# Left-over tokens of two experts share a tile: two column groups of the array, one expert in each

## The chip, the cores and the metric

The kernel runs on one core of one Trainium2 chip. The metric is the device time of one execution in microseconds (us). Times quoted are medians of the fast runs. A ratio is the mean time of one kernel's fast runs over that of the other's in the same rounds on the same chip, so it is not quite the ratio of the medians beside it. One profiled execution of each kernel gives the trace; what is told of a stage is read there.

## The reference, cut to what matters

Attention over 8 batches of 576 positions gives x, 4608 tokens of 512 features. Then each token goes to one of 8 experts, chosen by a gate and, for some tokens, inherited from the token before:

```python
for b in range(B):
    prev_e = -1
    for s in range(S):
        fresh_e = int(np.argmax(logits[b, s]))
        if s == 0 or local_gate[b, s] < 0.5:
            e = fresh_e
        else:
            e = prev_e if prev_e >= 0 else fresh_e
        prev_e = e
        # p = softmax(logits[b, s])
        h = np.maximum(x[b, s] @ w1[e], 0.0)      # 512 -> 1024
        out[b, s] = p[e] * (h @ w2[e])            # 1024 -> 512
```

All of it is float32. The weights of one expert are 2 x 2.1 MB.

## The kernel before

The kernel sorts the tokens by expert into tiles of 128. A tile holds tokens of one expert only, so each expert's count is rounded up to whole tiles. A first round of six tiles is made from the first three batches while attention still runs; the second round is routed during the first tiles. Each tile gathers its tokens, loads its expert's weights two tiles ahead into a ring of two, and runs two layers on TensorE (of a matmul's two operands, lhsT is called stationary and rhs moving). How many tiles there are is known only at run time; the last ones stand under an `If`.

```python
# route(): tiles of each expert, then small matmuls that spread the result
nc.vector.tensor_tensor(nti, ps[0:R, 0:1], nn[:, 0:1], op=Alu.add)     # count + 127
nc.vector.tensor_scalar(nti, nti, 7, None, Alu.arith_shift_right)
# ... cut ...
nc.tensor.matmul(ps[:, 0:n], lhsT=c.ones, rhs=over, start=True, stop=True)
# ... cut: for t in range(LT): slots of the tokens, six matmuls ...

# Experts
def hidden(self, j):                       # h transposed: W1 stationary, tokens move
    for g in range(FK // self.HB):
        ps = self.psh[2 * j + g]
        for i in range(self.HB):
            c = slice((g * self.HB + i) * P, (g * self.HB + i + 1) * P)
            for kk in range(DK):
                ins = nc.tensor.matmul(ps[:, i], lhsT=w1[:, kk, c], rhs=xT[:, kk * P:(kk + 1) * P],
                                       start=(kk == 0), stop=(kk == DK - 1))
        nc.scalar.activation(hT[:, g * self.HB:(g + 1) * self.HB], ps, Act.Relu)

def output(self, j):                       # tokens stationary, W2 moves
    for kk in range(FK):
        ins = nc.tensor.matmul(ps, lhsT=self.hT[j][:, kk], rhs=self.w2t[j][:, kk, :],
                               start=(kk == 0), stop=(kk == FK - 1))
    nc.scalar.activation(y, ps, Act.Copy, scale=self.pt[j])
    # ... cut: scatter of y to the output by an indirect DMA ...

def run(self, ctx, second, check):
    # ... cut ...
    for j in range(NT):
        ahead = self.weights(j + 2) if j + 2 < NT else []      # four pieces of 1 MB
        # ... cut: gather of tile j + 3; the last tiles under tc.If(used > ...) ...
        ins = self.hidden(j)
        for piece in ahead[:2]:
            piece()
        # ... cut: stages of the routing are put here while j < 3 ...
        if j + 1 < NT:
            self.turn_x(j + 1)             # four transposes
        ins = self.output(j)
        for piece in ahead[2:]:
            piece()
```

## Time and profile before

| what | value | read from |
|---|---|---|
| time | 773.4 us, 3 runs, 771.2 to 774.74 | runs |
| span of the profiled run | 775.6 us, granted clock 0.982 | core list |
| TensorE busy | 96% | page, part 1 |
| tiles run | 40 | matmul counts |
| one whole tile, start to start | 14.45 us | timeline |
| DMA in the expert stage (250 to 744 us) | share 0.91, 325 GB/s | windows |

A line of a costliest-groups list gives the source line, engine, operation, tile written and tiles read, shapes, count; then busy time and mean length of one; then the engine's idle time ahead of them and what ended it. Durations of matmuls overlap (a pass of the output layer lasts 0.59 us, and the next starts 0.43 us after it), so lengths of stages are taken from starts in the timeline. A line of a windows view gives the stretch and its length, then the busy time and number of instructions of PE (TensorE's matmuls), PEld (its weight loads), DVE (VectorE), ACT (ScalarE) and POOL (GpSimd), then the granted clock (the share of TensorE's full clock that it was given), the DMA share and GB/s. In float32 each matmul appears as two instructions, called passes (64 for the 32 matmuls of a hidden layer). The lines themselves are in the prediction.

### The profile page before, as it was taken

What the parts mean: (1) busy time and instruction counts of PE and PEld (TensorE: products, weight loads), DVE (VectorE), ACT (ScalarE), POOL (GpSimd) and SP (SyncE); (2) the same over time, 40 slices, a digit from 0 to 9 for tenths busy, and PEclk for the clock granted to TensorE, in tenths of its full rate; (3) what the DMA queues carried; (4) which work ended last, traced back from release to release, by engine and by line L of the source; (5) the groups of instructions that cost most, each with busy time, mean ns of one, the idle gap of its engine ahead of it and who ended that gap; (6) DMA issues with size and microseconds to landing.
All of it is one profiled execution on the core that took longest, in us unless ns stands there. A gap on an engine that the chain in (4) does not pass through costs nothing. (4 is left out here: it accounts for less than half of the span.)

```text
span 775.6 us, 13139 instructions
## 1 busy us (share of the span) xinstructions
PE 746.9 (96%) x5308; PEld 576.3 (74%) x5308; DVE 180.2 (23%) x599; ACT 151.9 (20%) x273; POOL 85.7 (11%) x104
## 2 busy tenths in 40 slices
PE   7999999999999999999999999999999999999990
PEld 7999889887777767767767767768768768768760
DVE  5677877753720000000000000000000000000000
ACT  2544434531101101101101101111111111111110
POOL 1000002001021111111111111111111111101100
PEclk9999979999999999999999999999999999999995
DMA  9888778886789899999899899899899899899892
GB/s 353 316 299 276 245 250 296 296 288 245 262 329 328 307 328 343 308 341 324 303 349 328 305 343 334 307 346 340 287 337 330 312 338 339 299 344 325 310 324 82
DMA packets 95977, 238.81 MB, mean 308 GB/s; under 512 B 10718, under 2 KB 19934, under 8 KB 95904
## 3 DMA queue, kind: packets, MB, share of 16 engines
q1 hardware_dynamic: 88736, 216.87, 79.5%
q0 software_dynamic: 6640, 20.89, 7.2%
q8 instruction: 46, 0.75, 0.4%
q14 instruction: 27, 0.22, 0.1%
q10 hardware_dynamic: 528, 0.07, 0.1%
HBM read 218.79 MB, written 20.07 MB: 308 GB/s over the span
## 5 line engine op out<-in xcount | busy, mean ns | idle before, releaser
L690 PEld LDWEIGHTS hps<-xgT,w1t 128*128 128x128 f32 x2560 | 291.7, 192 | 17.3 <-issue 16.7
L690 PE MATMUL hps<-xgT,w1t 128*128 128x128 f32 x2560 | 292.8, 275 | 0.3 <-DVE xgT L676 0.3
L699 PE MATMUL yps<-w2t,hT 128*128 128x512 f32 x640 | 281.3, 592 | 0.0
L699 PEld LDWEIGHTS yps<-w2t,hT 128*128 128x128 f32 x640 | 118.5, 190 | 133.9 <-issue 133.9
L676 DVE COPY xgT<-tps 128x512 f32<-128x512 f32 x41 | 28.3, 690 | 487.5 <-PE tps L675 487.3
L692 ACT ACTIVATE hT<-hps 128x512 f32<-128x512 f32 x80 | 47.8, 597 | 241.4 <-PE hps L690 238.4
L667 POOL DMA_INDIRECT xg<-xd,gi x43 | 42.0, 976 | 402.2 <-issue 144.9
L701 ACT ACTIVATE y<-yps,pt 128x512 f32<-128x512 f32 x40 | 27.5, 687 | 267.7 <-PE yps L699 267.7
L702 POOL DMA_INDIRECT out_dram<-y,si x40 | 40.5, 1011 | 268.0 <-ACT y L701 254.6
L315 PE MATMUL sps<-qt,kt 64*128 64x96 f32 (+2 forms) x704 | 50.7, 290 | 5.3 <-DMA kt<-in_k_dram 5.0
L315 PEld LDWEIGHTS sps<-qt,kt 64*128 64x128 f32 (+2 forms) x704 | 44.6, 197 | 10.0 <-issue 8.2
L319 ACT ACTIVATE e<-sps 128x576 f32<-128x576 f32 (+1 forms) x64 | 39.9, 651 | 19.4 <-PE sps L315 17.6
L362 PE MATMUL vps<-vlt,e 128*96 128x96 f32 x384 | 41.1, 265 | 0.0
L362 PEld LDWEIGHTS vps<-vlt,e 128*96 128x96 f32 x384 | 37.5, 177 | 3.9 <-issue 3.1
L362 PE MATMUL vps<-vst,e 108*108 108x108 f32 (+1 forms) x320 | 38.0, 274 | 1.0 <-DVE xs L373 0.8
L362 PEld LDWEIGHTS vps<-vst,e 108*108 108x108 f32 (+1 forms) x320 | 34.7, 185 | 2.7 <-PE vps L362 0.9
L322 DVE TENSOR_TENSOR e<-e,maskL 128x576 f32<-128x576 f32 x32 | 23.2, 753 | 18.3 <-ACT e L319 16.7
L322 DVE TENSOR_TENSOR e<-e,maskS 108x648 f32<-108x648 f32 (+1 forms) x32 | 23.1, 754 | 9.5 <-ACT e L319 9.5
L405 ACT COPY xT<-xps 128x324 f32<-128x324 f32 (+1 forms) x32 | 18.6, 683 | 33.0 <-PE xps L399 33.0
L675 PE MATMUL tps<-ident,xg 128*128 128x128 f32 x164 | 24.9, 273 | 0.0
L675 PEld LDWEIGHTS tps<-ident,xg 128*128 128x128 f32 x164 | 19.3, 142 | 0.1
L373 DVE TENSOR_TENSOR xl<-vps,rc 96x384 f32<-96x384 f32 x32 | 17.3, 545 | 0.5
(145 smaller groups left out, 230.9 us busy)
## 6 DMA issues: line engine op xcount, KB each, us to landing
w1t<-in_w_dram SPq DMA_DIRECT2D x84, 1024.0 KB
w2t<-in_w_dram SPq DMA_DIRECT2D x84, 1024.0 KB
kt<-in_k_dram SPq DMA_DIRECT2D x15, 608.0 KB
qt<-in_q_dram SPq DMA_DIRECT2D x15, 576.0 KB
vlt<-in_vl_dram SPq DMA_DIRECT2D x8, 780.0 KB
vst<-in_vs_dram SPq DMA_DIRECT2D x8, 650.0 KB
xd<-xl SPq DMA_DIRECT2D x8, 576.0 KB
xd<-xs SPq DMA_DIRECT2D x24, 108.0 KB
```

Source lines behind the costliest of these rows:

```text
L315: st["pe"] = nc.tensor.matmul(ps[0:kb, h, i * w:(i + 1) * w], lhsT=kt[r, u.i2, c:c + kb], rhs=qt[r, u.i2, c:c + w], start=True, stop=True)
L319: nc.scalar.activation(ev, ps[0:kb, :, 0:m * w], Act.Exp, bias=0.0, scale=1.0 / DH ** 0.5)
L322: nc.vector.tensor_tensor(blocks(ev, m), blocks(ev, m), mask, op=Alu.mult)
L362: nc.tensor.matmul(ps[0:w, o:o + w], lhsT=u.e[0:kb, h, i * w:(i + 1) * w], rhs=vt[0:kb, u.i2, u.t0 + i, c:c + w], start=True, stop=True)
L667: self.nc.gpsimd.indirect_dma_start(out=self.xg[j], out_offset=None, in_=self.xd[0:t["rows"]], in_offset=bass.IndirectOffsetOnAxis(ap=t["r ...
L675: nc.tensor.transpose(ps[:, kk * P:(kk + 1) * P], x[:, kk * P:(kk + 1) * P], self.c.ident)
L676: ins = nc.vector.tensor_copy(self.xT[j], ps)
L690: ins = nc.tensor.matmul(ps[:, i], lhsT=w1[:, kk, c], rhs=xT[:, kk * P:(kk + 1) * P], start=(kk == 0), stop=(kk == DK - 1))
L692: nc.scalar.activation(hT[:, g * self.HB:(g + 1) * self.HB], ps, Act.Relu)
L699: ins = nc.tensor.matmul(ps, lhsT=self.hT[j][:, kk], rhs=self.w2t[j][:, kk, :], start=(kk == 0), stop=(kk == FK - 1))
L701: nc.scalar.activation(y, ps, Act.Copy, scale=self.pt[j])
L702: nc.gpsimd.indirect_dma_start(out=self.out, in_=y, in_offset=None, bounds_check=N - 1, oob_is_err=False, out_offset=bass.IndirectOffsetOn ...
```

## The change

The intent: rounding up wastes rows. An expert whose left-over is at most 64 tokens now takes only half of a tile, and two such experts share one. For the mixed tile TensorE's array is used as two column groups of 64: each group holds the tokens of one half, and each expert's weights move through its own group. There are two mixed tiles (four halves), at fixed places 14 and 25 in the list, and so fewer whole ones. The second expert's weights go to a buffer of their own, in four pieces spread over four earlier tiles.

```diff
+HT = P // 2
+NM = 2
+NH = 2 * NM
+NT_MIN = (N - E * HT) // P
+NT_MAX = max((N + E * (P - HT - 1)) // P, N // P - 1 + E - NH)
+NT = NT_MAX + NM
+MIXED = (14, 25)
# ... cut; route(): one stage more, and three small matmuls more in a later one ...
+    if final:
+        few, rank, half = nn[:, 6:7], nn[:, 7:8], nn[:, 8:9]
+        nc.vector.tensor_tensor(few, nt, nts[:, 1:2], op=Alu.subtract)
+        ps = bank()
+        nc.tensor.matmul(ps[0:R, 0:1], lhsT=c.less[0:E, 0:R], rhs=few[0:E], start=True, stop=True)
# ... cut ...
+        yield
# ... cut ...
-    nc.tensor.matmul(ps[:, 0:n], lhsT=c.ones, rhs=over, start=True, stop=True)
+    nc.tensor.matmul(ps[:, 0:whole], lhsT=c.ones, rhs=over, start=True, stop=True)
     if final:
         nc.tensor.matmul(ps[0:1, n:n + 1], lhsT=c.ones[:, 0:1], rhs=nt[0:E], start=True, stop=True)
+        nc.tensor.matmul(ps[0:1, n + 1:n + 1 + NH], lhsT=c.er[0:E], rhs=whose, start=True, stop=True)
+        for h in range(2):
+            nc.tensor.matmul(ps[:, whole:n], lhsT=c.half[h], rhs=whose.rearrange("e (m h) -> e h m", h=2)[:, h],
+                             start=(h == 0), stop=(h == 1))
# ... cut; Experts ...
+    def hidden_mixed(self, j):
+        nc, xT = self.nc, self.xT[j]
+        for f in range(2):
+            ps = self.bank().rearrange("p a b -> p (a b)")
+            for kk in range(DK):
+                for h, w1 in enumerate((self.w1t[j], self.w1x)):
+                    nc.tensor.matmul(ps[h * HT:(h + 1) * HT], lhsT=xT[:, kk * P + h * HT:kk * P + (h + 1) * HT],
+                                     rhs=w1[:, kk, f * 512:(f + 1) * 512], start=(kk == 0), stop=(kk == DK - 1))
+            nc.scalar.activation(self.h[:, f * 512:(f + 1) * 512], ps, Act.Relu)
+        return self.turn_h(j, 0)
# ... cut: turn_h, four transposes of h and a copy to hT ...
     def output(self, j):
+        if "halves" in t:
+            self.turn_h(j, 1)
+            for kk in range(FK):
+                for h, w2 in enumerate((self.w2t[j], self.w2x)):
+                    s = slice(h * HT, (h + 1) * HT)
+                    ins = nc.tensor.matmul(ps[s], lhsT=self.hT[j][:, kk, s], rhs=w2[:, kk, :],
+                                           start=(kk == 0), stop=(kk == FK - 1))
# ... cut; run() ...
+            if j + 6 in MIXED:
+                extra = self.weights(j + 6, 1)
# ... cut ...
-            for piece in ahead[2:]:
+            for piece in ahead[2:] + extra[:1]:
                 piece()
+            extra = extra[1:]
```

The routing now spreads over four tiles instead of three, and the gathers of tiles 6 and 7 wait until tile 4.

More of the change, by code (lines that the diff above doesn't have):

```diff
@@ L41 @@
 GC = 32
-NT = (N + E * (P - 1)) // P
-NT_MIN = N // P
+HT = P // 2
[5 more added lines that the diff above has]
+MIXED = (14, 25)
 SKIP = 8192
@@ L92, with __init__ @@
 class Round:
-    def __init__(self, pool, n):
-        self.n = n
-        self.gi = pool.tile([P, n], I32, name="gi")
-        self.si = pool.tile([P, n], I32, name="si")
-        self.oh = pool.tile([P, n, E], F32, name="oh")
-        self.et = pool.tile([1, n + 1], I32, name="et")
+    def __init__(self, pool, whole, nm=0):
+        self.whole, self.n = whole, whole + nm
+        self.gi = pool.tile([P, self.n], I32, name="gi")
+        self.si = pool.tile([P, self.n], I32, name="si")
+        self.oh = pool.tile([P, self.n, E], F32, name="oh")
+        self.et = pool.tile([1, self.n + 1 + 2 * nm], I32, name="et")
 @with_exitstack
@@ L162, in __init__ @@
         nc.vector.memset(self.ones, 1.0)
+        self.half = []
+        for h in range(2):
+            t = pool.tile([E, P], F32, name=f"half{h}")
+            nc.vector.memset(t, 0.0)
+            nc.vector.tensor_scalar(t[:, h * HT:(h + 1) * HT], self.ones[:, 0:HT], er[0:E], None, Alu.mult)
+            self.half.append(t)
         _, self.io = const([P, P], [[1, P]], 0, 0, "io")
@@ L173, in passes @@
         r2 = ctx.enter_context(tc.tile_pool(name="slots2", bufs=1))
-        r2 = Round(r2, NT - NE)
+        r2 = Round(r2, NT_MAX - NE, NM)
         codes = keep.tile([LQ, LT, B, E], F32, name="codes")
@@ L486, in route @@
     nc = tc.nc
-    R, CN, n = nb * E, LT * nb, rd.n
+    R, CN, n, whole = nb * E, LT * nb, rd.n, rd.whole
     final = nb == B
@@ L516, in route @@
     nc.tensor.matmul(ps[0:R, 1:2], lhsT=c.before[0:R, 0:R], rhs=cnt, start=True, stop=True)
-    nn = rp.tile([R, 8], F32, name="nn")
+    nn = rp.tile([R, 12], F32, name="nn")
     if final:
@@ L524, in route @@
         nc.vector.memset(nn[:, 0:1], 0.0)
-    nti = rp.tile([R, 1], I32, name="nti")
-    nc.vector.tensor_tensor(nti, ps[0:R, 0:1], nn[:, 0:1], op=Alu.add)
+    nti = rp.tile([R, 2], I32, name="nti")
+    nc.vector.tensor_tensor(nti[:, 0:1], ps[0:R, 0:1], nn[:, 0:1], op=Alu.add)
+    nc.vector.tensor_scalar(nti[:, 1:2], nti[:, 0:1], -float(HT), None, Alu.add)
     nc.vector.tensor_scalar(nti, nti, 7, None, Alu.arith_shift_right)
-    nt = rp.tile([R, 1], F32, name="nt")
-    nc.vector.tensor_copy(nt, nti)
+    nts = rp.tile([R, 2], F32, name="nt")
+    nc.vector.tensor_copy(nts, nti)
+    nt = nts[:, 0:1]
     yield
+    if final:
[3 more added lines that the diff above has]
+        nc.tensor.matmul(ps[0:R, 0:1], lhsT=c.less[0:E, 0:R], rhs=few[0:E], start=True, stop=True)
+        nc.vector.tensor_copy(rank, ps[0:R, 0:1])
+        nc.vector.scalar_tensor_tensor(half, rank, float(NH), few, Alu.is_lt, Alu.mult)
+        nc.vector.tensor_tensor(nt, nt, half, op=Alu.subtract)
+        whose = rp.tile([E, NH], F32, name="whose")
+        nc.vector.tensor_scalar(whose, c.io[0:E, 0:NH], rank[0:E], half[0:E], Alu.is_equal, Alu.mult)
+        yield
     ps = bank()
@@ L546, in route @@
     nc.vector.tensor_tensor(end, first[0:E], tiles[0:E], op=Alu.add)
-    over = rp.tile([E, n], F32, name="over")
-    nc.vector.tensor_scalar(over, c.io[0:E, 0:n], end, None, Alu.is_ge)
+    over = rp.tile([E, whole], F32, name="over")
+    nc.vector.tensor_scalar(over, c.io[0:E, 0:whole], end, None, Alu.is_ge)
     thr, base = nn[:, 4:5], nn[:, 5:6]
@@ L559, in route @@
     nc.vector.scalar_tensor_tensor(slot, cum, base, slot, Alu.add, Alu.add)
+    if final:
+        last, far = nn[:, 9:10], nn[:, 10:11]
+        nc.vector.scalar_tensor_tensor(last, nt, float(P), thr, Alu.mult, Alu.add)
+        nc.vector.tensor_tensor(far, first, nt, op=Alu.add)
+        nc.vector.tensor_scalar(far, far, -float(P), float(P * whole), Alu.mult, Alu.add)
+        nc.vector.scalar_tensor_tensor(far, rank, float(HT), far, Alu.mult, Alu.add)
+        more = rp.tile([R, S], F32, name="more")
+        nc.vector.tensor_scalar(more, cum, last, far, Alu.is_gt, Alu.mult)
+        nc.vector.tensor_tensor(slot, slot, more, op=Alu.add)
     nc.vector.tensor_tensor(slot, slot, hot, op=Alu.mult)
@@ L564, in route @@
     ps = bank()
-    nc.tensor.matmul(ps[:, 0:n], lhsT=c.ones, rhs=over, start=True, stop=True)
+    nc.tensor.matmul(ps[:, 0:whole], lhsT=c.ones, rhs=over, start=True, stop=True)
     if final:
         nc.tensor.matmul(ps[0:1, n:n + 1], lhsT=c.ones[:, 0:1], rhs=nt[0:E], start=True, stop=True)
+        nc.tensor.matmul(ps[0:1, n + 1:n + 1 + NH], lhsT=c.er[0:E], rhs=whose, start=True, stop=True)
+        for h in range(2):
+            nc.tensor.matmul(ps[:, whole:n], lhsT=c.half[h], rhs=whose.rearrange("e (m h) -> e h m", h=2)[:, h],
+                             start=(h == 0), stop=(h == 1))
     sp = bank()
@@ L573, in route @@
     if final:
-        nc.vector.tensor_copy(rd.et[:, n:], ps[0:1, n:n + 1])
+        nc.vector.tensor_copy(rd.et[:, n:], ps[0:1, n:n + 1 + NH])
     nc.vector.tensor_tensor(rd.oh, across(c.io[:, 0:E], [P, n, E]), spread(ps[:, 0:n], [P, n, E]), op=Alu.is_equal)
@@ L647, in __init__, with weights @@
         self.pt = Ring(xp, 2, [P, 1], "pt")
-        self.T = [dict(rd=r1, i=i, rows=BE * S) for i in range(NE)] + [dict(rd=r2, i=i, rows=N) for i in range(NT - NE)]
-    def weights(self, j):
+        self.T = [dict(rd=r1, i=i, rows=BE * S) for i in range(NE)] + [dict(rd=r2, i=i, rows=N) for i in range(r2.whole)]
+        for m, j in enumerate(MIXED):
+            self.T.insert(j, dict(rd=r2, i=r2.whole + m, rows=N, halves=[r2.n + 1 + 2 * m + h for h in range(2)]))
+        self.used = 0
+    def weights(self, j, h=0):
         nc, t = self.nc, self.T[j]
@@ L654, in weights, with load @@
         w2 = lambda e: self.w2[bass.ds(e, 1)].rearrange("o (k p) f -> p (o k) f", p=P)
-        def load(dst, src, h):
-            if "e" not in t:
-                t["e"] = nc.values_load(t["rd"].et[0:1, t["i"]:t["i"] + 1], engines=[ET.SP], min_val=0, max_val=E - 1,
-                                        skip_runtime_bounds_check_because="a count of at most 8 experts, held to 7")
+        at = t["halves"][h] if "halves" in t else t["i"]
+        def load(dst, src, part):
+            if ("e", h) not in t:
+                t["e", h] = nc.values_load(t["rd"].et[0:1, at:at + 1], engines=[ET.SP], min_val=0, max_val=E - 1,
+                                           skip_runtime_bounds_check_because="an expert, from 0 to 7")
             k = dst.shape[1] // 2
-            nc.sync.dma_start(out=dst[:, h * k:(h + 1) * k], in_=src(t["e"])[:, h * k:(h + 1) * k])
-        return [lambda a=a, h=h: load(*a, h) for a in ((self.w1t[j], w1), (self.w2t[j], w2)) for h in range(2)]
+            s = slice(part * k, (part + 1) * k)
+            nc.sync.dma_start(out=dst[:, s], in_=src(t["e", h])[:, s])
+        to = ((self.w1x, w1), (self.w2x, w2)) if h else ((self.w1t[j], w1), (self.w2t[j], w2))
+        return [lambda a=a, part=part: load(*a, part) for a in to for part in range(2)]
     def gather(self, j):
@@ L680, in turn_x, with bank, turn_h @@
             nc.vector.tensor_reduce(self.pt[j], self.pe[j], axis=AX.X, op=Alu.add)
+    def bank(self):
+        self.used += 1
+        return self.psh[self.used - 1]
+    def hidden_mixed(self, j):
[8 more added lines that the diff above has]
+        return self.turn_h(j, 0)
+    def turn_h(self, j, f):
+        nc, ps = self.nc, self.bank()
+        for i in range(self.HB):
+            k = f * self.HB + i
+            ins = nc.tensor.transpose(ps[:, i], self.h[:, k * P:(k + 1) * P], self.c.ident)
+        nc.vector.tensor_copy(self.hT[j][:, f * self.HB:(f + 1) * self.HB], ps)
+        return ins.ins
     def hidden(self, j):
@@ L685, in hidden @@
         for g in range(FK // self.HB):
-            ps = self.psh[2 * j + g]
+            ps = self.bank()
             for i in range(self.HB):
@@ L697, in output @@
         ps, y = self.psy[j], self.y[j]
-        for kk in range(FK):
-            ins = nc.tensor.matmul(ps, lhsT=self.hT[j][:, kk], rhs=self.w2t[j][:, kk, :],
-                                   start=(kk == 0), stop=(kk == FK - 1))
+        if "halves" in t:
[5 more added lines that the diff above has]
+                                           start=(kk == 0), stop=(kk == FK - 1))
+        else:
+            for kk in range(FK):
+                ins = nc.tensor.matmul(ps, lhsT=self.hT[j][:, kk], rhs=self.w2t[j][:, kk, :],
+                                       start=(kk == 0), stop=(kk == FK - 1))
         nc.scalar.activation(y, ps, Act.Copy, scale=self.pt[j])
@@ L712, in run @@
         self.psy = Ring(pp, 2, [P, D], "yps")
+        xp = ctx.enter_context(tc.tile_pool(name="mixed", bufs=1))
+        self.w1x = xp.tile([P, DK, F], F32, name="w1x")
+        self.w2x = xp.tile([P, FK, D], F32, name="w2x")
+        self.h = xp.tile([P, F], F32, name="h")
+        steps = NE - AHEAD + 1
         used = None
+        extra = []
         self.turn_x(0)
-        for j in range(NT):
+        for j, t in enumerate(self.T):
             ahead = self.weights(j + 2) if j + 2 < NT else []
-            if j + AHEAD < NT:
-                self.gather(j + AHEAD)
+            for g in [] if j == steps - 1 else [NE, NE + 1] if j == steps else [j + AHEAD]:
+                if g < NT:
+                    self.gather(g)
             if j == NE and check:
                 check()
-            if j >= NT_MIN:
+            if j + 6 in MIXED:
+                extra = self.weights(j + 6, 1)
+            if t["rd"] is self.r2 and NT_MIN - NE <= t["i"] < self.r2.whole:
                 if used is None:
-                    et = self.r2.et
-                    used = self.nc.values_load(et[0:1, NT - NE:], min_val=NT_MIN - NE, max_val=NT - NE,
-                                               skip_runtime_bounds_check_because="the sum of the experts' tiles")
-                ctx.enter_context(tc.If(used > j - NE))
-            ins = self.hidden(j)
+                    at = self.r2.n
+                    used = self.nc.values_load(self.r2.et[0:1, at:at + 1], min_val=NT_MIN - NE, max_val=NT_MAX - NE,
+                                               skip_runtime_bounds_check_because="the sum of the experts' whole tiles")
+                ctx.enter_context(tc.If(used > t["i"]))
+            ins = (self.hidden_mixed if "halves" in t else self.hidden)(j)
             for piece in ahead[:2]:
                 piece()
-            if j < NE - AHEAD:
+            if j < steps:
                 with tc.issue_after(ins):
                     next(second, None)
-                    if j == NE - AHEAD - 1:
-                        next(second, None)
             if j + 1 < NT:
@@ L737, in run @@
             ins = self.output(j)
-            for piece in ahead[2:]:
+            for piece in ahead[2:] + extra[:1]:
                 piece()
-            if j < NE - AHEAD:
+            extra = extra[1:]
+            if j < steps:
                 with tc.issue_after(ins):
```

## The prediction

> **What bounds the kernel now.** I read the page's busy rows and costliest groups first, then the windows of 50 us, then the timeline of one tile, then the DMA queue's issues.
>
> ```profile
> PE 746.9 (96%) x5308; PEld 576.3 (74%) x5308; DVE 180.2 (23%) x599; ACT 151.9 (20%) x273; POOL 85.7 (11%) x104
> ...
> L690 PE MATMUL hps<-xgT,w1t 128*128 128x128 f32 x2560 | 292.8, 275 | 0.3 <-DVE xgT L676 0.3
> L699 PE MATMUL yps<-w2t,hT 128*128 128x512 f32 x640 | 281.3, 592 | 0.0
> ```
>
> The two expert matmul groups hold 574 us of a 775.6 us span, with 0.3 us of idle ahead of them. A whole tile is 64 instructions of L690 and 16 of L699 (32 and 8 matmuls in float32, two passes each), so 2560/64 = 640/16 = 40 tiles ran. Busy times of matmuls overlap, so I take starts from the timeline of one tile in the middle (start, length, engine):
>
> ```profile
> 407.59 7.31 PE L690 MATMUL hps<-xgT,w1t 128*128 128x128 f32 x64
> ...
> 414.74 0.60 PE L675 MATMUL tps<-ident,xg 128*128 128x128 f32 x4
> ...
> 415.17 7.03 PE L699 MATMUL yps<-w2t,hT 128*128 128x512 f32 x16
> ...
> 422.04 7.31 PE L690 MATMUL hps<-xgT,w1t 128*128 128x128 f32 x64
> ```
>
> From start to start: hidden layer 414.74 - 407.59 = 7.15 us (112 ns a pass), four transposes 0.43 us, output layer 422.04 - 415.17 = 6.87 us (429 ns a pass of 512 columns). A tile is **14.45 us**, and the next begins at once. The other possible bound is the weights: 4.19 MB a tile. Windows of 1 us in that tile (the columns at the end are granted clock, DMA share, GB/s):
>
> ```profile
> 402.00:403.00 1.00, 1.00 (x4) 0.51 (x3) 0.00 (x0) 0.00 (x0) 0.57 (x1) 1.00 1.05 422
> ...
> 414.00:415.00 1.00, 1.00 (x12) 1.00 (x11) 0.00 (x0) 0.00 (x1) 0.00 (x0) 1.00 0.36 141
> ```
>
> ```profile
> 400.04 0.99 SPq L661 DMA_DIRECT2D w1t<-in_w_dram  x2
> 404.35 3.81 SPq L661 DMA_DIRECT2D w2t<-in_w_dram  x2
> 414.49 1.03 SPq L661 DMA_DIRECT2D w1t<-in_w_dram  x2
> ```
>
> The DMA is near full in the middle of a tile and falls off at its end, until a hidden layer frees the next w1 buffer: the queue waits for TensorE, not the reverse. The two are close (window 400:450: DMA share 0.90, 325 GB/s), so both must be checked. Adding up the packets of the weight queue, I find the last w2 piece of that tile landing at 416.4, the second w1 piece issued at 415.15 landing at 422.1, and its tile starting at 436.5: **14 us of slack**.
>
> [...] the gate matmuls (L415) put four results into four groups of 32 columns.
>
> ```profile
> 50.49 0.64 PEld L415 LDWEIGHTS xps<-xT,wgs 128*32 128x32 f32 x16
> 50.49 1.18 PE L415 MATMUL xps<-xT,wgs 128*32 128x288 f32 x16
> ```
>
> Sixteen passes of 288 columns one after the other would take 16 x 429 x 288/512 = 3.86 us; they took 1.18 us, and the starts come in fours, about 7 ns apart, 243 ns from four to four. So in this very data type the groups overlap fully[...]. [...] In the trace the matmul after the gates starts 0.09 us later than the last four's 243 ns would allow; I book 0.1 us a switch. [...] the trace shows 390 to 440 while pieces queue behind each other.
>
> **The change part by part.**
>
> *Tiles.* Running the reference's routing on its inputs gives 701, 469, 606, 495, 656, 452, 546 and 683 tokens for the eight experts; left over after whole tiles of 128: 61, 85, 94, 111, 16, 68, 34, 43. Rounded up that is 40 tiles, as the profile has. Experts 0, 4, 6 and 7 have at most 64 left over: exactly the four halves of two mixed tiles. So 36 whole and 2 mixed tiles: **four whole tiles (57.80 us) are replaced by two mixed ones.**
>
> *A mixed tile on TensorE.* The hidden layer swaps operands: the 64 tokens of each half are stationary, W1 moves in 512 columns. 2 x 4 x 2 = 16 matmuls, 32 passes, in pairs on two column groups: 16 slots x 429 ns = 6.87 us. The output layer is 16 matmuls in pairs likewise: 6.87 us. The hidden result is now tokens by features and needs eight transposes besides the four of the next x: 3 x 0.43 = 1.29 us. Four mode switches: 0.4 us. Waits: the second ReLU ends about 0.1 + 0.6 us after its last matmul, and the first transposes and those of x (0.86 us) stand between; the first hT copy (0.69 us on VectorE) is covered by the second transposes. I book 0.2 us. Sum 6.87 + 6.87 + 1.29 + 0.4 + 0.2 = **15.6 us**. Gain: 57.80 - 2 x 15.6 = 26.6 us. ACT and VectorE do two more PSUM passes of 0.6 to 0.7 us in these tiles, on engines over 80% idle there.
>
> *Routing.* The first three tiles carry it:
>
> ```profile
> 170.09 7.41 PE L690 MATMUL hps<-xgT,w1t 128*128 128x128 f32 x64 [0.35 <-DVE xgT L676]
> ...
> 186.54 7.41 PE L690 MATMUL hps<-xgT,w1t 128*128 128x128 f32 x64
> ...
> 203.10 7.41 PE L690 MATMUL hps<-xgT,w1t 128*128 128x128 f32 x64
> ...
> 219.35 7.38 PE L690 MATMUL hps<-xgT,w1t 128*128 128x128 f32 x64
> ```
>
> They take 16.45, 16.56 and 16.25 us: 5.9 us over three plain tiles. The change adds one stage (one small matmul) and three more small matmuls in the last; in the instruction order they all stand between tile halves, behind VectorE work that is done by then. Small ones here cost 0.15 to 0.35 us: **+0.7 us**. The gathers of tiles 6 and 7 move to tile 4, after the index table; that table is then ready near 236 us, and tile 6 is transposed near 257 us. Off the path.
>
> *Weights.* 36 + 4 = 40 expert loads plus the two run-ahead ones: the same 168 MB-sized pieces. The second expert's four pieces go out one per tile in tiles 8 to 11 and 19 to 22. Such a tile carries five pieces. Queued pieces land about 3.15 us apart, so 15.8 us against 14.45: the queue falls behind some 1.3 us a tile, 5.4 us in all, then recovers over seven tiles. 5.4 is under 14, so TensorE should not wait. Two gathers and two scatters go (1 MB).
>
> Sum: 26.6 - 0.7 = 25.9 us. **773.4 - 25.9 = 747.5 us** (-3.3%); the profiled span should be near 750.
>
> **The rivals.** (a) The pairs run in sequence: each mixed tile then costs 13.7 us more, 27 us, all of the gain: 774 us. For it: here the pairs accumulate over 4 or 8 steps in interleaved order, which the gates don't, and groups are 64 wide. Against it: the gates' overlap in float32, in one bank. 4%. (b) DMA becomes the bound: the same bytes in 26 us less, about 189 MB (40 loads, 38 gathers and scatters) over some 549 us = 344 GB/s, against some 390 when queued. It would show as waits of L768 or of the mixed tiles for weights and cost perhaps 3 to 12 us: 751 to 760. For it: a share of 0.90 to 0.95 already. Against: 14 us of slack, and the share falls off only where the queue has nothing to send. 10%. (c) The mixed tile's chain (ReLU, transpose, copy) shows openly: 1 to 2 us each, 750 us.
>
> **Range and chances.** The middle case carries perhaps 1.5 us of its own error (switches, waits, routing) and the three runs of before spread over 3.5 us. Range 743.5 to 753. 2% faster is 757.9: only (a) and the bad end of (b) reach it. Faster 0.94, same 0.055, slower 0.005.
>
> **What would show it.** 72 ReLUs into hT and four into the new h; mixed tiles of 15.6 us from start to start; 16 starts of pairs 429 ns apart in each layer; whole tiles still at 14.45; DMA share near 0.95 and about 344 GB/s in the expert stage. Wrong if the mixed tiles are near 29 us (a), if whole tiles 9 to 14 or 20 to 25 stretch with waits for w1t or w2t (b), or if tile 6 waits for its gather.

## The result, and the profile after

The changed kernel took **750.83 us** in the median (four runs, 743.36 to 751.97) against 772.3 for the kernel before; the ratio is 0.9701, with a 95% interval of 0.963 to 0.9773. In a later job of five rounds on one chip (six runs of it) the same code took 746.98 us (742.85 to 751.54) against 775.0, ratio 0.9657. The spread of one kernel's runs is part of the story below.

From the page of the changed kernel, the busy row and the two groups of the whole tiles:

```profile
PE 722.9 (96%) x5132; PEld 546.1 (73%) x5132; DVE 183.8 (25%) x614; ACT 148.3 (20%) x267; POOL 84.4 (11%) x100
...
L768 PE MATMUL hps<-xgT,w1t 128*128 128x128 f32 x2304 | 263.8, 275 | 0.3 <-DVE xgT L730 0.3
L785 PE MATMUL yps<-w2t,hT 128*128 128x512 f32 x576 | 254.9, 596 | 0.0
```

2304/64 = 576/16 = 36 whole tiles, and TensorE is as busy as before: it still sets the end, with fewer tiles to do. The timeline of the first mixed tile of the changed kernel (start, length, line, operands):

```profile
381.31 0.64 PE L747 MATMUL hps<-w1t,xgT 128*64 128x512 f32 x1
381.32 0.64 PE L747 MATMUL hps<-w1x,xgT 128*64 128x512 f32 x1
381.79 0.59 PE L747 MATMUL hps<-w1t,xgT 128*64 128x512 f32 x1
381.80 0.59 PE L747 MATMUL hps<-w1x,xgT 128*64 128x512 f32 x1
382.22 0.59 PE L747 MATMUL hps<-w1t,xgT 128*64 128x512 f32 x1
382.23 0.59 PE L747 MATMUL hps<-w1x,xgT 128*64 128x512 f32 x1
...
388.33 0.66 PE L756 MATMUL hps<-ident,h 128*128 128x128 f32 x4
388.82 0.60 PE L729 MATMUL tps<-ident,xg 128*128 128x128 f32 x4
389.26 0.60 PE L756 MATMUL hps<-ident,h 128*128 128x128 f32 x4
389.84 0.64 PE L781 MATMUL yps<-w2t,hT 128*64 128x512 f32 x1
389.85 0.64 PE L781 MATMUL yps<-w2x,hT 128*64 128x512 f32 x1
...
396.86 7.41 PE L768 MATMUL hps<-xgT,w1t 128*128 128x128 f32 x64
```

A pass of one expert (w1t) and one of the other (w1x) start within 0.01 us of each other. The second pair follows the first after 0.48 us, and each later one after the 0.43 us that a lone pass of 512 columns takes. Both experts go through the array in the time of one. Hidden layer 7.02 us, twelve transposes 1.51 us, output layer 7.02 us: **15.55 us** to the next tile's start (15.54 us in the second mixed tile).

The two profiles, cut at the same places of TensorE's timeline:

| stretch | before | after | difference |
|---|---|---|---|
| to the start of tile 0 | 170.09 | 170.06 | -0.03 |
| tiles 0 to 3, with the routing | 63.79 | 66.27 | +2.48 |
| tile 4 to the start of the last output layer | 513.65 | 487.41 | -26.24 |
| from there to the end | 28.03 | 26.43 | -1.60 |
| span | 775.55 | 750.16 | -25.39 |

The second row holds something that no part of the prediction had. Windows of the changed kernel around the routing of tile 2 (the columns at the end are granted clock, DMA share and GB/s):

```profile
209.00:212.00 3.00, 3.00 (x29) 2.72 (x28) 0.92 (x5) 0.60 (x1) 0.00 (x0) 0.99 0.64 216
212.00:215.40 3.40, 3.40 (x5) 1.35 (x4) 3.40 (x6) 0.00 (x0) 0.00 (x0) 0.50 1.02 418
```

For 3.4 us the granted clock is 0.50, right after a row of small routing matmuls (209.05 to 211.20 us):

```profile
209.05 0.40 PE L608 MATMUL xps<-over,ones 8*128 8x33 f32 x2
...
210.08 1.18 PE L618 MATMUL xps<-inb,run 64*96 64x8 f32 x12
211.20 0.66 PE L729 MATMUL tps<-ident,xg 128*128 128x128 f32 x4
211.69 8.73 PE L785 MATMUL yps<-w2t,hT 128*128 128x512 f32 x16
```

The output layer of tile 2 takes 8.57 us from start to start instead of 6.87: 1.70 of the 2.48 us. The rest, 0.78 us, is the small matmuls.

### The profile page after: what moved, and what is told of

It is laid out like the page before. It is cut to its first block, busy times and chain, and to the rows that moved or that the text cites.

```text
span 750.2 us, 12762 instructions
## 1 busy us (share of the span) xinstructions
PE 722.9 (96%) x5132; PEld 546.1 (73%) x5132; DVE 183.8 (25%) x614; ACT 148.3 (20%) x267; POOL 84.4 (11%) x100
## 5 line engine op out<-in xcount | busy, mean ns | idle before, releaser
L768 PEld LDWEIGHTS hps<-xgT,w1t 128*128 128x128 f32 x2304 | 262.4, 192 | 16.0 <-issue 15.5
L768 PE MATMUL hps<-xgT,w1t 128*128 128x128 f32 x2304 | 263.8, 275 | 0.3 <-DVE xgT L730 0.3
L785 PE MATMUL yps<-w2t,hT 128*128 128x512 f32 x576 | 254.9, 596 | 0.0
L785 PEld LDWEIGHTS yps<-w2t,hT 128*128 128x128 f32 x576 | 107.2, 191 | 121.6 <-issue 121.6
L770 ACT ACTIVATE hT<-hps 128x512 f32<-128x512 f32 x72 | 43.0, 597 | 216.3 <-PE hps L768 208.7
L721 POOL DMA_INDIRECT xg<-xd,gi x41 | 40.3, 983 | 381.2 <-issue 139.0
L391 DVE TENSOR_TENSOR xl<-vps,rc 96x384 f32<-96x384 f32 x32 | 17.3, 545 | 0.5
```

The costliest lines, as they stand in the source:

```text
L721: self.nc.gpsimd.indirect_dma_start(out=self.xg[j], out_offset=None, in_=self.xd[0:t["rows"]], in_offset=bass.IndirectOffsetOnAxis(ap=t["r ...
```

## The experiments

Each changed the kernel given in its text and gave a correct result. The profiled runs are compared stage by stage, in the stretches of the table above, since a chance in the first stretch (below) moves the time as a whole by up to 7 us.

### 1. One half after the other

```diff
-            for kk in range(DK):
-                for h, w1 in enumerate((self.w1t[j], self.w1x)):
+            for h, w1 in enumerate((self.w1t[j], self.w1x)):
+                for kk in range(DK):
# ... the same in output() ...
```

> The same mixed tiles, but all matmuls of one half stand ahead of all those of the other, so neighbours in the stream share a column group. Theory (the gain is the overlap of neighbours in different column groups, and TensorE starts matmuls in the order of the stream): only the passes at the seams overlap, 29 slots of 0.429 us in the hidden layer and 31 in the output layer where there were 16 and 16, so a mixed tile takes 15.55 + 28 x 0.429 = 27.6 us and the whole about 775 us (751 + 24). Rival (the engine finds the overlap in any order, or the gain does not come from it): 751 us, mixed tiles still 15.6 us.

Measured: 758.92 us in the median, ratio to before 0.9794; a mixed tile takes 22.62 us, the stretch from tile 4 is 14.15 us longer than in the changed kernel. Both expectations missed. The order matters, so the gain is the overlap; but here matmuls did not start strictly in the order of the stream either: the second half's first pass starts at 376.27 us, ahead of three passes of the first half at 376.69, 377.12 and 377.55. Timeline of this kernel:

```profile
374.49 2.36 PE L747 MATMUL hps<-w1t,xgT 128*64 128x512 f32 x5
376.27 0.64 PE L747 MATMUL hps<-w1x,xgT 128*64 128x512 f32 x1
376.69 0.59 PE L747 MATMUL hps<-w1t,xgT 128*64 128x512 f32 x1
...
384.90 5.79 PE L781 MATMUL yps<-w2t,hT 128*64 128x512 f32 x13
390.10 0.64 PE L781 MATMUL yps<-w2x,hT 128*64 128x512 f32 x1
```

In the hidden layer eight passes of the first half stand ahead (the order of the stream is that of the kernel's text; the trace does not record it), and the second half starts when five have started; in the output layer it is 13 of 16. Both times three passes of the first half are still to start. In the changed kernel the second half starts beside the first pass; here it starts 1.78 and 5.20 us later, after 4 and 12 passes more, 16 x 0.43 = 6.9 us. Measured are 22.62 - 15.54 = 7.1.

### 2. Halves in blocks

Two matmuls (four passes) of one half, then two of the other in the hidden layer; four and four in the output layer.

```diff
-            for kk in range(DK):
-                for h, w1 in enumerate((self.w1t[j], self.w1x)):
+            for k2, h, kk in [(a, h, 2 * a + b) for a in range(DK // 2) for h in range(2) for b in range(2)]:
# ... in output(), blocks of four: 4 * a + b, for b in range(4) ...
```

> Halves in blocks: in the hidden layer two matmuls (four passes) of one half, then two of the other; in the output layer four (eight passes) and four. The run with the halves in turn gave 22.62 us a mixed tile, neither of the two numbers expected: the second half's first pass started when three passes of the first half's row were still to start. [...] Then blocks of four passes overlap fully and blocks of eight leave four slots of 0.43 us: 15.54 + 0 + 1.72 = 17.3 us a mixed tile. Rival (starts strictly in the order of the stream): nine slots more in the hidden layer and thirteen in the output layer, 25 us. The time as a whole: about 4 us over the changed kernel, or 19 us.

Measured (one run): 750.58 us, and 17.48 us a mixed tile, against 17.3 and 25 expected. In the output layer, with blocks of eight passes, the second half starts 1.77 us after the first, when five of eight have started and three are still to start, as in experiment 1. In the hidden layer, with blocks of four, it starts 0.01 us after the first. The count came from one run and foretold another. What in the engine makes it is not shown.

### 3. The routing alone

```diff
-        nc.vector.scalar_tensor_tensor(half, rank, float(NH), few, Alu.is_lt, Alu.mult)
+        nc.vector.scalar_tensor_tensor(half, rank, 0.0, few, Alu.is_lt, Alu.mult)
-MIXED = (14, 25)
+MIXED = ()
# ... and the numbers of tiles as before ...
```

> The new routing stages run, but no expert gets a half: 40 whole tiles, no mixed ones. Theory (routing costs 0.8 us of small matmuls plus 1.7 us because the longer row of small matmuls in tile 2 lets the granted clock fall to half for one window of 3.4 us): 2.5 us slower than before, about 774.8 us against 772.3, with a half-clock window near 212 us in the profile. Rival (the half-clock window was chance): 0.8 us slower, no such window. Either way no gain may be left: all of it is to come from the tiles.

Measured: 776.53 us against 774.47, ratio 1.0001 (0.9941 to 1.0061), which by itself tells nothing apart. The profile does: tiles 0 to 3 take 66.37 us, 2.58 more than before (2.5 expected), with a half-clock window of 3.4 us at 207.2 us. The stretch from tile 4 is 513.72 us, as before. No part of the gain is in the routing, and the window comes with it.

### 4. One mixed tile

```diff
-NM = 2
+NM = 1
-MIXED = (14, 25)
+MIXED = (14,)
```

> One mixed tile instead of two: 39 tiles. Theory (each mixed tile is worth 28.90 - 15.75 = 13.15 us, routing costs 2.5 us once): 772.3 - 10.7 = 761.6 us. Rival (the two mixed tiles get in each other's way through the weight queue, or the first is worth more than the second): some other split than half of the gain, for example 756 or 766 us.

Measured: 759.31 us against 774.47, ratio 0.982. In the profile the stretch from tile 4 takes 500.57 us: 13.08 less than before, and 13.16 more than with two. Each mixed tile is worth the same, 13.1 us, and the two don't disturb each other.

### 5. How much room the weights have

A spare buffer takes one more piece of weights (or two) after the output layer of each of the tiles 6 to 31.

```diff
+            if NE <= j < 32:
+                for a in range(1):
+                    self.nc.sync.dma_start(out=self.wz[a], in_=self.w2[bass.ds(t["e", 0], 1)].rearrange(
+                        "o (k p) f -> p (o k) f", p=P)[:, 0:FK // 2])
```

> One more piece of weights (1 MB, read again into a spare buffer) in each of the tiles 6 to 31: 5.8 MB a tile or 399 GB/s at 14.45 us, and six pieces in the eight tiles that carry the second expert's. Theory (the weights have some 14 us of slack, and five pieces a tile just about keep pace, as in tiles 8 to 11 of the changed kernel, where the queue lost some 0.3 us a tile): 8 x about 2.6 us + 18 x about 0.2 us = 24 us behind by tile 23, of which 14 are slack: 5 to 12 us slower than the changed kernel. Rival (the DMA is the bound already): every added MB costs, 26 x 2.6 = 68 us slower. Rival (there is far more room): no change.

Measured with one piece: 756.85 us, ratio to before 0.9786. The stretch from tile 4 is 10.05 us longer than in the changed kernel (5 to 12 expected), of which 1.7 are a half-clock window at 516 us that followed the waits. TensorE's waits for weights:

```profile
PE hps L768 <- DMA w1t<-in_w_dram: 3.6, 5, 1.4
PE hps L747 <- DMA w1t<-in_w_dram: 1.5, 1, 1.5
```

The columns are the time waited, the number of waits and the longest. 26 MB more than in the changed kernel were loaded, and TensorE waited 5.1 us for weights in all. The other 3.2 us of the 10.05 are not broken down.

> Two more pieces in each of the tiles 6 to 31: 6.8 MB a tile. Here the DMA must become the bound, and the length of a whole tile between 24 and 31 gives its rate: at 400 to 410 GB/s a tile takes about 16.8 us, and the whole some 60 us more than the changed kernel, with waits of the hidden layer for w1t.

Measured with two pieces (one run): 827.48 us, and 51.1 us of waits of the hidden layer for w1t. The stretch from tile 4 is 80.4 us longer; 17 of them are half-clock windows (34 us at half the clock) that follow TensorE's waits, which I had not counted. Some 9 us of the 80.4 are in neither. The window of 590 to 700 us gives the rate when the DMA is the bound:

```profile
590.00:700.00 110.00, 95.24 (x521) 61.94 (x520) 7.00 (x21) 11.98 (x19) 12.95 (x13) 1.00 1.04 396
```

396 GB/s, where the expert stage of the changed kernel (250 to 720 us) runs at 343. Windows of the changed kernel over the tiles that carry the second expert's weights, and over the plain ones after:

```profile
310.00:367.00 57.00, 57.00 (x332) 41.69 (x331) 3.71 (x12) 6.87 (x12) 7.97 (x8) 1.00 1.03 395
410.00:460.00 50.00, 50.00 (x303) 37.68 (x302) 2.78 (x9) 6.93 (x11) 6.99 (x7) 1.00 0.92 326
```

In four tiles the DMA moves 395 GB/s, as much as where it was the bound (396), and TensorE does not wait, being busy for all 57 us.

### 6. The row of small matmuls cut in two

In the changed kernel the counts, experts and slots of the tokens make one row of 2.15 us of small matmuls between the hidden layer of tile 2 and its transposes. Here the slots come after the output layer; a later stage is merged, so the routing ends where it did.

```diff
+    nc.vector.tensor_tensor(rd.oh, ...)          # moved up, with the copies to rd.et
+    if final:
+        yield
     sp = bank()
     sps = sp[0:LQ, 0:CN].rearrange("p (t b) -> p t b", b=nb)
     for t in range(LT):
         nc.tensor.matmul(sps[:, t], lhsT=slot[...], rhs=c.inb[0:R, 0:nb], start=True, stop=True)
# ... cut ...
-    yield
+    if not final:
+        yield
```

> The changed kernel with the row of small routing matmuls in tile 2 cut in two: the counts and experts after its hidden layer (about 1.0 us), the slots after its output layer (about 1.1 us); the same work, the same end of the routing. Theory (a row of 2.15 us of small matmuls lets the granted clock fall): no half-clock window near 212 us, the output layer of tile 2 back at 6.9 us, 1.7 us faster than the changed kernel, about 749. Rival (chance, or a cause elsewhere): the window stays or moves, 750.8 us.

Measured: 744.64 us (six runs, 741.95 to 750.22), ratio to before 0.961. No half-clock window in tile 2; tiles 0 to 3 take 64.76 us, 1.51 less than uncut. Its profile had a window of 13.7 us at 100.9 us, and its runs spread over 8 us, so the other window was still there.

### 7. A longer row in the kernel before; the row moved

```diff
+    if final:
+        for _ in range(3):
+            nc.tensor.matmul(ps[:, n + 1:n + 3], lhsT=c.ones, rhs=c.io[0:E, 0:2], start=True, stop=True)
```

> The kernel before with three dummy matmuls (8 rows, 128 columns, 2 results) added to its row of small routing matmuls between tiles 1 and 2, which grows from 1.56 to about 2.4 us. Theory (a row over some 2 us starts a half-clock window): a window of 3.4 us near 204 us, tile 2 about 1.7 us longer, 2.5 us in all. Rival (the window has another cause, such as the transposes right after the row or the added routing stage): 0.9 us more and no window.

Measured: 774.26 us against 775.0, ratio 0.9991. The row was 2.3 us long, and no window followed. So the length alone does not do it. Next, the changed kernel with its uncut row at such a place:

```diff
+    if final:
+        yield
     ps = bank()
     nc.tensor.matmul(ps[:, 0:whole], lhsT=c.ones, rhs=over, start=True, stop=True)
# ... and the later yield only if not final ...
```

> The changed kernel with its uncut row of small routing matmuls one place later: after the output layer of tile 2, ahead of a hidden layer, no longer ahead of the four transposes. The row lengthened in the kernel before, at such a place, had no half-clock window. Theory 1 (what counts is the row of 2.15 us and the four transposes behind it, 2.6 us together): no window here. Theory 2 (the row alone does it, and the lengthened row of the kernel before escaped by how it fell): a window of 3.4 us near its end, at 211 to 219 us.

Measured: 746.6 us (four runs, 741.3 to 749.33), ratio to before 0.9633; a window of 3.4 us at 216.7 us. The transposes are not needed. Windows of this kernel, then of the kernel before with the longer row:

```profile
213.30:216.70 3.40, 3.40 (x27) 2.44 (x26) 0.72 (x4) 0.69 (x1) 0.98 (x1) 1.00 1.04 355
216.70:220.10 3.40, 3.40 (x18) 3.40 (x18) 3.37 (x6) 0.00 (x0) 0.00 (x0) 0.50 0.94 349
```

```profile
198.70:202.10 3.40, 3.40 (x13) 1.56 (x12) 0.00 (x0) 0.58 (x1) 0.00 (x0) 1.00 1.03 398
202.10:205.50 3.40, 3.40 (x33) 3.36 (x33) 2.25 (x8) 0.10 (x1) 1.00 (x1) 1.00 1.02 344
```

In the profiles all changes of the clock lie at whole multiples of 3.413 us from each other: 26, 3, 29, 1 and 152 of them in the changed kernel, 26, 3 and 189 in the kernel before. This gives a grid of slots and its place in each run; it falls differently on the program from run to run (the first routing's window starts at 102.74 us in the one and at 103.01 in the other). The question is then how much of a row falls into one slot of the grid:

| profile | row of small matmuls, us | largest part in one slot, us | half-clock window after that slot |
|---|---|---|---|
| changed kernel, two profiles | 2.15 | 2.15 | yes, both |
| halves in turn; one mixed; blocks; two more pieces | 2.15 | 2.14 to 2.15 | yes, all four |
| routing alone | 2.15 | 2.11 | yes |
| row moved | 2.14 | 2.14 | yes |
| one more piece a tile | 2.14 | 1.56 | no |
| before, longer row | 2.3 | 1.63 | no |
| before | 1.56 | 1.10 | no |
| row cut: three profiles | 1.03 and 1.11, apart | 1.11 | no |

Eight of eight with 2.1 us or more in one slot had the window, six of six with 1.6 us or less had none. The cleanest pair is the changed kernel and the one with one more piece, which differ only from tile 6 on: the same row at the same place in the program, 2.15 us of it in one slot with the window and 1.56 us without, and 66.27 and 64.56 us for tiles 0 to 3. The profile, in which the ends of matmuls are modelled, shows TensorE busy without a gap at this row (3.40 of 3.40 us in the slots above, 3.00 of 3.00 in the changed kernel): no wait of TensorE stood ahead of the window here. For this row no profile lies between 1.6 and 2.1 us. At the first routing's row (experiment 8), 1.16 us or more in one slot was followed by the window in nine profiles of nine, 1.08 us or less in none of five, so no one length parts the profiles at both rows.

In all 14 profiles 38 slots at full clock were followed by a half-clock one: nine at the first row, eight at the row of tile 2, seven that held TensorE's waits for weights (experiment 5) and the 14 ends of the programs. What these have in common was not tested.

### 8. Both rows cut, and the changed kernel beside it

> The changed kernel itself once more, as the measure for the two runs beside it. The profiles so far show two kinds of half-clock window ahead of the end: one near 103 us whose length differs from run to run (0, 3.4, 10.2 or 13.7 us, in kernels whose attention is the same), and one of 3.4 us in tile 2 in all four profiles with the uncut row of small routing matmuls (this one, halves in turn, routing alone, one mixed), in none without it. If the first is chance and the second is not: times from about 743 to 752 us, a window of 3.4 us near 205 to 212 us in the profile again.

Measured: 746.98 us (six runs, 742.85 to 751.54), ratio 0.9657; window of 3.4 us at 204.0 us, none near 103.

The first routing, inside the attention, has a shorter such row at 100 to 102 us. Cutting it too needs one line:

```diff
-    if final:
-        yield
+    yield
     sp = bank()
# ... and no later yield ...
```

> As the run with the cut row, and the first routing, which runs inside the attention, has its row cut in the same way (counts at one place, slots one place later). Theory A (the window near 103 us is also started by a row of small matmuls, which stand at 100 to 102 us): no window there, tile 0 starts at 163 us in every run, times near 741 to 743 us with little spread. Theory B (that window comes from the attention around it, or by chance): windows of 0 to 13.7 us as before, times from 741 to 750 us as with the cut row alone.

Measured: **743.82 us** (six runs, 742.5 to 744.79), ratio to before 0.9603 (0.957 to 0.9637). No window but that at the very end, granted clock 0.989 to 0.991 in all six runs, and a spread of 2.3 us where the changed kernel had 8.7 in the same job. Windows of the kernel before, then of this one:

```profile
103.00:113.30 10.30, 10.30 (x63) 9.41 (x62) 5.14 (x19) 2.44 (x4) 0.00 (x0) 0.50 0.56 185
```

```profile
103.00:113.30 10.30, 10.30 (x132) 9.05 (x131) 9.05 (x29) 5.27 (x10) 0.00 (x0) 1.00 0.74 249
```

At full clock 132 matmuls fit into the same 10.3 us, at half clock 63. The chance window of 0 to 13.7 us, worth up to 6.8 us, was the main source of the spread in the changed kernel. Whether it starts went with how much of the row lay in one slot (nine of nine against none of five, experiment 7); what sets its length is not shown. The kernel before has the same window (10.2 us in its profile), and its runs of this job fit: clock 0.989 in those of 769.2 and 771.5 us, 0.981 to 0.986 in those above 774 us. Part of this ratio is therefore a gain that the kernel before could have as well; no run measured it.

### 9. No loads for tiles that do not run

Weights are loaded two tiles ahead, also for two tiles that turn out not to exist. This puts those loads under an `If`, on top of the version with both rows cut.

```diff
+            def pieces(some):
+                if used is not None and some:
# ... cut: the expert's number is read here ...
+                    with tc.If(used > self.T[j + 2]["i"]):
+                        for piece in some:
+                            piece()
```

> As the run with both rows cut, and the last tiles load weights two tiles ahead only where that tile will run, so the 8 MB for tiles 38 and 39, which do not run, are not loaded. Theory: the end of the program waits behind these loads (a branch on TensorE that takes 6.8 us after the last tile, and loads that land 9.6 us after it), so the tail after the start of the last output layer falls from 26.4 us by about 5 us, to some 21; the tiles keep 14.45 us. Rival: the tail is fixed work (drains, semaphores) and stays at 25 to 26 us; or the extra branches cost the tiles time.

Measured: **741.65 us** (six runs, 740.79 to 742.52), ratio to before 0.958 (0.9547 to 0.9613). The stretch after the start of the last output layer is 22.76 us, 3.13 less than with both rows cut; 5 were expected. (In the other profiles of kernels with two mixed tiles it is 24.67 to 26.43 us, so one pair gives the size only roughly; the medians differ by 2.2 us.) The tiles keep their 14.45 us. This version beats both kernels.

## Why the prediction was right

The time fell inside the range by the chain of reasons it gave; two terms of the sum were mis-sized. That the middle case came so close in the profiles (25.9 us expected, 25.39 measured) is luck: 1.8 us that the routing cost more were made up by 1.6 us in the tail that nobody had foreseen.

- **The bound.** TensorE set the end before and after; busy 96% both times.
- **Tiles.** 36 whole and two mixed tiles ran, as counted; 72 ReLUs into hT and four into h, as said.
- **A mixed tile.** 15.6 us foretold, 15.55 and 15.54 measured. The two layers took 0.15 us more each than their passes, the transposes 0.22 more than their 1.29; switches and waits together came to 0.5 us of the 0.6 booked. The neighbours' layers take another 0.2 us a mixed tile. Expected 26.6 us of gain, measured 26.24 in the stretch from tile 4.
- **Routing, mis-sized.** "+0.7 us" was right for the small matmuls (0.78, and 0.77 in the profile of experiment 5 whose row had no window). The term left out the 3.4 us at a granted clock of 0.50 that followed the fuller row: 1.70 us more. In experiments 3, 6 and 7 it came with the row, in eight profiles of eight with 2.1 us or more of it in one slot, and in none of six with 1.6 us or less.
- **Weights, mis-sized without effect.** The queue was to fall 5.4 us behind. The first w1 piece of a tile lands 4.4 us after its issue in plain tiles and 5.8 us in the worst of the four loaded ones: 1.4 us behind. A fifth piece mostly fills the gap at the end of a tile, where the DMA share fell to 0.36 (over the loaded tiles the share is 1.03, over plain ones 0.92), and that gap had not been put into the sum. Experiment 5 bears out that there is slack: it took 26 MB more, with six pieces in eight of the tiles, to bring 5.1 us of waits.
- **Tail.** Taken as unchanged; the profile has 1.6 us less. Two profiles of the changed kernel itself differ as much (26.43 and 24.67 us). Experiment 9 shows that the tail contains 2 to 3 us behind loads that nobody needs; why it differs between profiles is not shown.
- **The rivals.** (a), pairs in sequence, is refuted by the timeline; experiment 1 shows what a poorer order costs, 7.1 us a mixed tile. (b), the DMA as the bound, did not occur: the profile of the changed kernel has no wait of TensorE for weights, and even with 26 MB more (experiment 5) it waited 5.1 us in all. (c), an open chain of ReLU, transpose and copy, is at most the 0.2 us that were booked.
- **The range.** Of the ten runs of the changed kernel two (743.36 and 742.85) lie just under its low end. The profile of the second has no window near 103 us and the first ran at a clock of 0.987, against 0.98 in the other three of its job: the chance window fits both. The prediction had taken the spread from three runs of before, without a cause.

## What to carry to other kernels

Where rounding up to 128 wastes rows of a bound TensorE, two tenants with at most 64 rows each can share the array as two column groups at little more than the price of one (15.54 us here against 14.45), if their matmuls alternate in the stream (with blocks of four passes the hidden layer of experiment 2 still took 7.07 us, against 7.02). Before spending such a gain on the weights' side, ask what the DMA does in its idle gap: a queue at 0.91 that only pauses for buffers took another 1 MB in each of eight tiles without a wait. And look at the granted clock in windows of a few microseconds: here a row of 2.15 us of small matmuls was followed by 3.4 us at a clock of 0.50, which made the large ones after it 1.70 us longer, and cut into rows of 1.03 and 1.11 us it was not, so try spreading such rows between large matmuls.
